# Turning the cluster similarities and the one-hot words on VectorE instead of on TensorE and by DMA

## The chip, the cores and the metric

The kernel runs on one core of one Trainium2 chip. The time is device time in microseconds (us) of that core for one execution. Before the change three runs gave 378.12, 378.9 and 383.21 us, a median of 378.9.

## The reference, cut to what matters

Two stages follow each other. The first is attention in which a query sees only the keys of its own cluster; the second is a gate with a long convolution, done by Fourier transforms (as matmuls in the kernel). The change lies in how the first finds the clusters.

```python
B, H, S, D, n_clusters = 4, 8, 768, 64, 16
q_assign = argmax(einsum('bhsd,hcd->bhsc', q_n, c_n), axis=-1)   # nearest of 16 centroids
k_assign = argmax(einsum('bhsd,hcd->bhsc', k_n, c_n), axis=-1)
mask     = q_assign[:, :, :, None] == k_assign[:, :, None, :]
scores   = where(mask, scale * q @ k.T, -1e9)
attn     = softmax(scores) @ v                                   # ties go to the first centroid
x        = attn, heads side by side                              # (4, 768, 512)
x1,x2,x3 = split(x @ w_proj)
out      = (x1 * irfft(rfft(x2) * rfft(filter)) * x3) @ w_out
```

The kernel makes no mask matrix. Each query and key gets 16 more rows beside its 64 features: a one-hot word of its cluster. A key's word is 1 at its cluster and 0 elsewhere, a query's is 0 at its cluster and a large negative number elsewhere, so the score matmul adds the mask by itself.

## The kernel before, in words

The 32 pairs of batch and head are worked in eight groups (n = 0 to 7) of four heads, each group in two pairs of heads (pr). `attention(n, pr)` (L677) runs over six tiles of 128 keys: TensorE (PE) makes the scores (L694, with the helper lines L82 and L84), ScalarE (ACT) their exponentials (L708, L711) into one of five p buffers, PE multiplies these with v (L718 to L725), and VectorE (DVE) adds them up for the denominators (L743; the first two tiles in thirds, on DVE or GpSimd (POOL), L739). `hyena(b)` (L831) is the second stage for batch b; its pieces are put between the attention of later groups, and the last batch's stand alone at the end. In it DVE multiplies spectra (L887), POOL or DVE combines them (L891), DVE and POOL unfold the inverse (L956, L966) and gate it (L969), and PE multiplies with w_out; the results go to `out` by DMAs of SP (L1012), two row tiles at a time (512 KB), except the very last tiles (L1008, L989).

`routing(n)` (L574) prepares group n, while group n - 1 is in attention:

- PE transposes raw q and k (L594), copies go to qkP (L282 on ACT, L284 on DVE), and casts of these to the bf16 tiles aug (L610, done on ACT, DVE or POOL).
- L625: 8 matmuls give the similarities in two PSUM banks, 128 partitions (4 blocks of 32: queries and keys of two pairs, 16 centroids for each of two heads) by 2 x 384 columns of tokens.
- L630: two copies, 128x384 fp32, by ACT or DVE, to the tile sim.
- L638: PE turns them with six fp32 128x128 transposes into two more banks, so that tokens lie on partitions.
- L646 and L648: DVE takes the maximum over 16 centroids and compares, from PSUM, once for each bank, into the tile oh.
- L651, L659, L663: ties are broken towards the first centroid (multiply by a falling weight, largest of 16 in four halvings), and the words made: L663 in two halves, `is_equal` for keys and `subtract` for queries.
- L668: one DMA transpose on SP turns oh back into ohT, with tokens along the row.
- L497, in `masks` (L490): eight DMAs on SP put rows of ohT into aug. The scores of group n wait for these.

Group 0 has its own path (`first_masks`, L502) and is left as it is.

The order on each engine is not the order of the code. `Plan.place` (L123) sorts all operations by a list schedule: each has an engine with a duration or several to choose from, what it reads and writes, and a due time. `NUDGE` (L42) shifts the due time of each operation, and `ONLY` (L43) pins 121 of them to an engine. The result is one fixed list for each engine. An operation with `lock` on POOL waits for the last such one on DVE. SP issues its DMAs in its own list's order, and each queue goes on only when its next entry is free to go.

Of the kernel before, what the change touches and what calls it, by code (L numbers as in the profile page):

```python
# [264 lines left out]
def build(T):  # L265
# [25 lines left out]
    def bank(i):  # L291
        return T.bank[i][:]
# [10 lines left out]
    def dma(e):  # L303
        return (T.nc.scalar if e == "ACT" else T.nc.sync).dma_start
# [269 lines left out]
    def routing(n):  # L574
# [54 lines left out]
        for ch in range(2):  # L629
            op(EV384, lambda e, ch=ch, h=h: copy(e, T.sim[:, ch], bank(h.ids[ch])[:, :384]), b0 + 1.4 + .1 * ch, r=[h],  # L630
               w=[("sim", ch, 0), ("sim", ch, 1)], free=[h])
        SIM = [("sim", ch, pr) for ch in range(2) for pr in range(2)]
        h = Bank(cls, 2)
        both = lambda x: [(x, 0), (x, 1)]

        def simT(e, h=h):
            for i in range(NT):
                T.nc.tensor.transpose(bank(h.ids[i // 3])[:, ts(i % 3, 128)], T.sim[:, i // 3, ts(i % 3, 128)],  # L638
                                      T.ident)
        op(("PE", .72), simT, b0 + 2.5, r=SIM + ["ident"], w=[h], alloc=h)  # L640

        words = lambda: T.oh[:].rearrange("p a n c -> p (a n c)").rearrange("p (m c i) -> p m c i", c=NC, i=4)
        for ch in range(2):
            sv = lambda ch=ch, h=h: bank(h.ids[ch])[:, :384].rearrange("p (m i c) -> p m i c", i=4, c=NC)
            mx = lambda ch=ch: T.mx[:, ch].rearrange("p (m i) -> p m i", i=4)
            op(("DVE", .55), lambda e, sv=sv, mx=mx: V().tensor_reduce(mx(), sv(), axis=AX, op=Alu.max),  # L646
               b0 + 3.3 + .2 * ch, r=[h], w=[("mx", ch)])
            op(("DVE", .55), lambda e, ch=ch, sv=sv, mx=mx: V().tensor_tensor(  # L648
                words()[:, 6 * ch:6 * ch + 6], sv().rearrange("p m i c -> p m c i"), mx().unsqueeze(2).to_broadcast([128, 6, NC, 4]),
                op=Alu.is_equal), b0 + 3.4 + .2 * ch, r=[h, ("mx", ch)], w=[("oh", ch)], free=[h])  # L650
# [627 lines left out]
```

## Time and profile before

| | |
|---|---|
| median of three runs | 378.9 us |
| the profiled execution | 378.54 us |
| its span on the core | 376.8 us |
| granted clock of PE, mean | 0.995 |
| PE busy | 363.2 us, 96% |
| DVE busy | 341.1 us, 91% |
| ACT busy | 263.9 us, 70% |
| POOL busy | 113.7 us, 30% |
| six transposes of L638, once for each of groups 1 to 7 | 42 matmuls of 273 ns (median), 0.81 to 0.82 us for six |
| DMA transposes of L668 | 7, of 1.25 to 1.69 us on SP, 2.8 us to landing |

A line of a group reads: the line of the kernel, engine and operation, what it writes and reads (partitions by elements, type), how often, then busy time in us, mean ns of one, and the idle time of the engine just before with what ended it. PE is TensorE's matmuls and PEld its weight loads, which lie beside them. A busy PE in this table is not the same as a PE at its peak, since the ends of matmuls are modelled. The chain of work that ended last goes back from the last instruction, at each step to what released it.

### The profile page before, as it was taken

Reading aid. Unit: us, or ns where it says so; the run is one execution under the profiler, and the core shown is the slowest. Engines: PE = TensorE matmul, PEld = TensorE weight load, DVE = VectorE, ACT = ScalarE, POOL = GpSimd, SP = SyncE. Lnnn points to the kernel's source line nnn. Section 1 sums busy time; section 2 is a strip of 40 time slices with the busy share of each in tenths; the row PEclk is TensorE's granted clock in tenths of the full one; section 3 lists DMA queues with packets and bytes.
Section 4 is the critical chain, followed back from the end, with each engine's and each line's share of the span. In section 5 each row is a group of like instructions: output and inputs, shape, how many; then the busy total and the mean of one; then the engine's idle time right before and its main releaser. Section 6 shows DMA issues by size and latency. Waiting matters only on the chain.

```text
span 376.8 us, 8529 instructions
## 1 busy us (share of the span) xinstructions
PE 363.2 (96%) x3253; PEld 209.1 (55%) x3257; DVE 341.1 (91%) x509; ACT 263.9 (70%) x492; POOL 113.7 (30%) x156
## 2 busy tenths in 40 slices
PE   6899998999999999999999999999999999999994
PEld 3454553554555664556556656576555666565672
DVE  7778997979999999998999998999998999999993
ACT  6997868984992879688869538878773588333332
POOL 8441103141204452122441134433121433024610
PEclk9899999999999999999999999999999999999999
DMA  9959669855766858539894877646467733110304
GB/s 171 167 138 199 107 139 224 177 105 116 178 139 125 174 68 169 67 103 179 148 149 130 150 176 175 145 64 90 75 115 179 144 66 69 46 43 0 159 11 167
DMA packets 95716, 47.56 MB, mean 126 GB/s; under 512 B 83816, under 2 KB 89660, under 8 KB 95676
## 3 DMA queue, kind: packets, MB, share of 16 engines
q1 hardware_dynamic: 91052, 37.39, 43.5%
q0 software_dynamic: 2752, 8.98, 16.8%
q10 hardware_dynamic: 1872, 0.66, 0.7%
q8 instruction: 25, 0.41, 0.5%
q14 instruction: 15, 0.12, 0.2%
HBM read 31.59 MB, written 7.40 MB: 103 GB/s over the span
## 4 chain that ended last, share of the span: by engine, by line
PE 69%; DVE 13%; ACT 7%; DMA 4%; issue 3%; SPq 2%; POOL 1%; DVEq 0%; POOLq 0%; ACTq 0%
PE pair L722 28%; PE bank L84 24%; PE bank L594 5%; PE bank L82 3%; PE bank L625 2%; PE bank L857 2%; DMA dn<-dd 2%; PE bank L638 2%; DVE tm L887 1%; DVE tm L871 1%; ACT aug L282 1%; SPq L497 1%; DMA aug<-ohT 1%; ACT p L711 1%; DMA dd<-acc 1%
## 5 line engine op out<-in xcount | busy, mean ns | idle before, releaser
L722 PE MATMUL pair<-p,vraw 128*64 128x385 f32 x768 | 142.4, 489 | 0.0
L711 ACT ACTIVATE p<-bank 128x512 f32<-128x512 f32 x192 | 108.5, 610 | 23.0 <-PE bank L84 20.2
L743 DVE TENSOR_TENSOR acc<-p,acc 128x1536 f32<-128x1536 f32 x64 | 113.5, 1774 | 10.9 <-POOL acc L739 5.8
L722 PEld LDWEIGHTS pair<-p,vraw 128*64 128x64 f32 x768 | 55.8, 136 | 46.3 <-issue 39.1
L84 PE MATMUL bank<-aug,aug 128*64 128x512 bf16 (+3 forms) x650 | 70.7, 325 | 1.4 <-DMA aug<-ohT 0.5
L708 ACT ACTIVATE p<-bank 128x512 f32<-128x512 f32 x96 | 57.9, 608 | 11.0 <-PE bank L84 8.3
L84 PEld LDWEIGHTS <-aug 128*64 128x64 bf16 (+1 forms) x650 | 39.6, 109 | 35.2 <-issue 24.8
L776 POOL DMA_DIRECT2D acc<-acc x30 | 23.7, 791 | 93.5 <-DMA acc<-acc 45.2
L84 PE MATMUL bank<-xT,wpj 128*64 128x384 bf16 x456 | 43.3, 326 | 0.0
L84 PEld LDWEIGHTS <-wpj 128*64 128x64 bf16 x456 | 27.7, 110 | 13.7 <-issue 5.2
L284 POOL CAST aug<-qkP 64x768 bf16<-64x768 f32 x23 | 19.3, 842 | 52.3 <-DVE acc L743 21.0
L739 POOL TENSOR_TENSOR acc<-p,p 128x512 f32<-128x512 f32 x14 | 18.1, 1297 | 48.5 <-DVE acc L739 26.0
L282 ACT COPY qkP<-bank 128x512 f32<-128x512 f32 (+1 forms) x47 | 23.8, 555 | 12.6 <-PE bank L594 8.7
L84 PEld LDWEIGHTS <-y 128*64 128x64 bf16 x472 | 23.8, 110 | 13.1 <-issue 4.0
L887 DVE TENSOR_TENSOR tm<-bank,hm 128x512 f32<-128x512 f32 x44 | 28.0, 680 | 1.5 <-POOL y L891 0.8
L891 POOL TENSOR_TENSOR y<-tm 128x512 bf16<-128x512 f32 x17 | 21.5, 1277 | 20.2 <-DVE tm L887 12.3
L282 ACT CAST aug<-qkP 64x768 bf16<-64x768 f32 x28 | 23.1, 830 | 1.4 <-PE bank L84 0.6
L84 PE MATMUL bank<-wout,y 128*64 128x512 bf16 (+1 forms) x200 | 23.4, 371 | 0.2 <-DVE y L969 0.2
L746 ACT COPY osb<-pair 128x770 f32<-128x770 f32 x16 | 12.9, 804 | 14.6 <-PE pair L722 14.4
L739 DVE TENSOR_TENSOR acc<-p,p 128x512 f32<-128x512 f32 x34 | 22.6, 693 | 0.3 <-ACT p L711 0.3
L857 PE MATMUL bank<-wpj,xT 128*64 128x512 bf16 x192 | 22.0, 379 | 0.0
L282 ACT COPY ob<-bank 128x512 f32<-128x512 f32 x20 | 11.1, 590 | 15.1 <-PE bank L84 13.1
(174 smaller groups left out, 457.8 us busy)
## 6 DMA issues: line engine op xcount, KB each, us to landing
vraw<-in_v_dram SPq DMA_DIRECT2D x16, 384.0 KB, 3.8
qkraw<-in_q_dram SPq DMA_DIRECT2D x30, 192.0 KB, 4.1
rb<-dr SPq DMA_DIRECT2D x30, 192.0 KB, 3.7
out_dram<-ob SPq DMA_DIRECT2D x11, 512.0 KB, 4.1
qkraw<-in_k_dram SPq DMA_DIRECT2D x29, 192.0 KB, 4.4
acc<-acc POOLq DMA_DIRECT2D x10, 384.0 KB, 5.0
acc<-acc POOLq DMA_DIRECT2D x10, 192.0 KB, 4.0
y<-in_moe_filter_fft_dram SPq DMA_DIRECT2D x4, 384.0 KB, 6.7
```

The costliest lines, as they stand in the source:

```text
L84: T.nc.tensor.matmul(out[64 * i:64 * i + 64], lhsT[:, 64 * i:64 * i + 64], rhs, start=start, stop=stop)
L282: T.nc.scalar.copy(out, in_)
L284: (T.nc.vector if e == "DVE" else T.nc.gpsimd).tensor_copy(out, in_)
L708: T.nc.scalar.activation(o, ap(h).rearrange("p (a b) -> p a b", a=2), Act.Exp, scale=0.125)
L711: T.nc.scalar.activation(flat(s)[:, lo:lo + 512], ap(h), Act.Exp, scale=0.125)
L722: T.nc.tensor.matmul(o[64 * hp:64 * hp + 64, ch, :385], T.vraw[vs][:, hp, sk * D:(sk + 1) * D], T.p[slots[sk]][:, hp, 384 * ch:384 * ch + ...
L739: alu(e).tensor_tensor(o, x, y, op=Alu.add)
L743: T.nc.vector.tensor_tensor(T.acc[os], T.p[slots[sk]][:, :, :S], T.acc[os], op=Alu.add)
L776: op(("POOL", .8), lambda e, rows=rows: T.nc.gpsimd.dma_start(flat_()[:rows], flat_()[rows:2 * rows], accum_op=Alu.add), te, r=[], w=AK, b ...
L857: T.nc.tensor.matmul(ap(h)[64 * i:64 * i + 64], T.xT[xs][:, kt, c:c + 64], T.wpj[:, kt, DM:2 * DM], start=kt == 0, stop=kt == ND - 1)
L887: op(("DVE", .68), lambda e, i=i, cs=cs, r=r, h=h: T.nc.vector.tensor_tensor(T.tm[r][:, cs], ap(h), hmrow(i, (0, 2, 2, 3)[2 * r + cs]), op ...
L891: op({"POOL": 1.5, "DVE": .68}, lambda e, i=i, r=r: alu(e).tensor_tensor(T.y[:, i, r], T.tm[r][:, 0], T.tm[r][:, 1], op=Alu.add if r else ...
```

## The change

For groups 1 to 7, tokens are no longer brought onto all 128 partitions. DVE transposes blocks of 32 by 32: two transposes read the similarities in PSUM and write sim, so that each block of 32 partitions holds 32 tokens, with their 16 centroids times two heads along the row. The views (`turned`) put the four blocks of 128 tokens side by side, so one step from centroid to centroid is four elements in sim and in oh. The copies of the similarities, the six PE transposes and their two banks go. The maximum and the comparison are made once over 768 elements, from sim in SBUF. The last step of the words is one `subtract` for queries and keys. A third DVE transpose turns oh into ohT in place of the DMA transpose, and a comparison with zero makes the keys' rows (partitions 64 to 127) 0 or 1. The rows that `masks` reads become 16 neighbouring partitions, where they were every fourth one.

In the last batch, the third and fourth output tiles are stored one by one as the fifth was, by SP or ACT.

`NUDGE` has new values for all operations, so that the order on every engine is new, and `ONLY` pins 96 in place of 121.

```diff
-NUDGE = {0:-457.288,1:-646.784,2:-12.57, ...
-ONLY = {10:"POOL",12:"POOL",13:"POOL", ...
+NUDGE = {0:-746.767,1:-4870.897,2:-1.564, ...
+ONLY = {10:"POOL",11:"POOL",13:"POOL", ...
@@ masks
-                    rows = slice(64 * j + 2 * pr + hp, 64 * j + 64, 4) if n else slice(64 * pr + 32 * j + 16 * hp, 64 * pr + 32 * j + 16 * hp + 16)
+                    rows = slice(*((64 * j + 32 * pr if n else 64 * pr + 32 * j) + 16 * hp + x for x in (0, 16)))
@@ routing
+        turned = lambda x, g: x.rearrange("p (g x i) -> p g i x", g=g, i=4)
         for ch in range(2):
-            op(EV384, lambda e, ch=ch, h=h: copy(e, T.sim[:, ch], bank(h.ids[ch])[:, :384]), b0 + 1.4 + .1 * ch, r=[h],
-               w=[("sim", ch, 0), ("sim", ch, 1)], free=[h])
+            op(("DVE", .55), lambda e, ch=ch, h=h: V().transpose(
+                turned(T.sim[:, ch], 3), bank(h.ids[ch])[:, :384].rearrange("p (g i x) -> p g i x", g=3, i=4)), b0 + 1.4 + .1 * ch,
+               r=[h], w=[("sim", ch, 0), ("sim", ch, 1)], free=[h])
-        h = Bank(cls, 2)
-        def simT(e, h=h):
-            for i in range(NT):
-                T.nc.tensor.transpose(bank(h.ids[i // 3])[:, ts(i % 3, 128)], T.sim[:, i // 3, ts(i % 3, 128)],
-                                      T.ident)
-        op(("PE", .72), simT, b0 + 2.5, r=SIM + ["ident"], w=[h], alloc=h)
-        words = lambda: T.oh[:].rearrange("p a n c -> p (a n c)").rearrange("p (m c i) -> p m c i", c=NC, i=4)
-        for ch in range(2):
-            sv = lambda ch=ch, h=h: bank(h.ids[ch])[:, :384].rearrange("p (m i c) -> p m i c", i=4, c=NC)
-            mx = lambda ch=ch: T.mx[:, ch].rearrange("p (m i) -> p m i", i=4)
-            op(("DVE", .55), lambda e, sv=sv, mx=mx: V().tensor_reduce(mx(), sv(), axis=AX, op=Alu.max),
-               b0 + 3.3 + .2 * ch, r=[h], w=[("mx", ch)])
-            op(("DVE", .55), lambda e, ch=ch, sv=sv, mx=mx: V().tensor_tensor(
-                words()[:, 6 * ch:6 * ch + 6], sv().rearrange("p m i c -> p m c i"), mx().unsqueeze(2).to_broadcast([128, 6, NC, 4]),
-                op=Alu.is_equal), b0 + 3.4 + .2 * ch, r=[h, ("mx", ch)], w=[("oh", ch)], free=[h])
+        flat3 = lambda x: x.rearrange("p (m c i) -> p m c i", c=NC, i=4)
+        sims = lambda: flat3(T.sim[:].rearrange("p a b -> p (a b)"))
+        words = lambda: flat3(T.oh[:].rearrange("p a n c -> p (a n c)"))
+        mx = lambda: T.mx[:].rearrange("p a (m i) -> p (a m) i", i=4)
+        op(("DVE", .93), lambda e: V().tensor_reduce(mx(), sims().rearrange("p m c i -> p m i c"), axis=AX, op=Alu.max),
+           b0 + 3.3, r=SIM, w=both("mx"))
+        op(("DVE", .93), lambda e: V().tensor_tensor(
+            words(), sims(), mx().unsqueeze(2).to_broadcast([128, 12, NC, 4]), op=Alu.is_equal), b0 + 3.4,
+           r=SIM + both("mx"), w=both("oh"), lock=True)
...
-        for j, o_ in ((1, Alu.is_equal), (0, Alu.subtract)):
-            op(("DVE", .36), lambda e, j=j, o_=o_: V().tensor_tensor(
-                words()[:, j::2], words()[:, j::2],
-                T.mt[:, :48].rearrange("p (m i) -> p m i", i=4)[:, j::2].unsqueeze(2).to_broadcast([128, 6, NC, 4]), op=o_),
-               b0 + 4.2, r=both("m2"), w=both("oh"), lock=True)
+        op(("DVE", .56), lambda e: V().tensor_tensor(
+            words(), words(), T.mt[:, :48].rearrange("p (m i) -> p m i", i=4).unsqueeze(2).to_broadcast([128, 12, NC, 4]),
+            op=Alu.subtract), b0 + 4.2, r=both("m2"), w=both("oh"), lock=True)
-        op(("SP", .6), lambda e: T.nc.sync.dma_start_transpose(
-            T.ohT[:].rearrange("p (t n) -> p t n", n=128), T.oh[:].rearrange("p a n c -> p (a n c)")), due - 2,
-           r=both("oh"), w=both("ohT"), byts=196e3, lat=3.0 if n < 3 else 1.0)
+        op(("DVE", .93), lambda e: V().transpose(
+            T.ohT[:].rearrange("p (g i x) -> p g i x", g=6, i=4), turned(T.oh[:].rearrange("p a n c -> p (a n c)"), 6)), due - 2,
+           r=both("oh"), w=both("ohT"), lock=True)
+        op(("DVE", .35), lambda e: V().tensor_scalar(T.ohT[64:], T.ohT[64:], 0.0, None, op0=Alu.is_equal), due - 1, r=[],
+           w=both("ohT"), lock=True)
@@ hyena
-                if last and tt == 2 and not e_:
-                    op(("SP", .4), lambda e, tt=tt, e_=e_, ob=ob: T.nc.sync.dma_start(
+                if last and tt and not (tt == 2 and e_):
+                    op({"SP": .4, "ACT": .4}, lambda e, tt=tt, e_=e_, ob=ob: dma(e)(
                         T.out[b].rearrange("(p t) m -> p t m", t=NT)[:, 2 * tt + e_], ob()[:, e_]), due + 2,
                        r=[obk[e_]], byts=157e3)
-            if not (last and tt == 2):
+            if not (last and tt):
...
-                   r=obk, byts=320e3)
+                   r=obk, byts=400e3)
```

More of the change, by code (lines that the diff above doesn't have):

```diff
@@ L43 @@
-ONLY = {10:"POOL",12:"POOL",13:"POOL",14:"POOL",15:"POOL",26:"SP",27:"SP",30:"SP",32:"ACT",34:"SP",38:"ACT",41:"ACT",50:"DVE",62:"ACT",64:"POOL",69:"POOL",90:"DVE",91:"POOL",94:"DVE",97:"DVE",98:"POOL",173:"POOL",174:"DVE",175:"DVE",223:"DVE",224:"DVE",229:"DVE",230:"POOL",235:"DVE",241:"ACT",242:"POOL",245:"ACT",323:"DVE",355:"POOL",357:"POOL",392:"ACT",405:"POOL",406:"DVE",408:"POOL",410:"DVE",411:"DVE",412:"DVE",414:"DVE",415:"POOL",419:"ACT",460:"POOL",462:"POOL",497:"DVE",512:"DVE",539:"DVE",547:"DVE",550:"DVE",563:"DVE",573:"ACT",580:"ACT",588:"ACT",595:"ACT",599:"DVE",607:"POOL",617:"ACT",687:"ACT",688:"ACT",689:"ACT",690:"DVE",692:"POOL",693:"DVE",695:"ACT",696:"DVE",697:"ACT",698:"POOL",699:"POOL",700:"ACT",701:"POOL",703:"DVE",704:"DVE",807:"POOL",808:"DVE",860:"ACT",861:"ACT",870:"ACT",915:"DVE",916:"DVE",988:"POOL",1010:"ACT",1048:"DVE",1051:"ACT",1066:"DVE",1068:"ACT",1095:"POOL",1146:"POOL",1147:"POOL",1152:"DVE",1154:"POOL",1155:"ACT",1156:"DVE",1312:"ACT",1313:"DVE",1314:"DVE",1315:"POOL",1317:"ACT",1372:"DVE",1419:"DVE",1424:"ACT",1452:"POOL",1492:"ACT",1500:"ACT",1505:"POOL",1519:"DVE",1603:"ACT",1604:"ACT",1605:"ACT",1610:"POOL",1611:"POOL",1612:"POOL",1770:"POOL",1772:"DVE",1882:"DVE",1889:"DVE",1934:"DVE",1939:"ACT",1942:"ACT"}
@@ new lines @@
+ONLY = {10:"POOL",11:"POOL",13:"POOL",15:"POOL",28:"SP",30:"ACT",31:"SP",33:"SP",35:"SP",41:"ACT",50:"DVE",62:"DVE",69:"POOL",92:"POOL",96:"DVE",98:"DVE",150:"DVE",173:"POOL",174:"DVE",175:"DVE",224:"POOL",229:"DVE",230:"DVE",235:"ACT",236:"POOL",241:"POOL",242:"ACT",354:"POOL",389:"ACT",402:"POOL",403:"ACT",404:"DVE",407:"DVE",409:"DVE",411:"ACT",412:"DVE",413:"POOL",454:"POOL",455:"POOL",456:"POOL",491:"DVE",556:"DVE",570:"DVE",578:"ACT",585:"DVE",604:"ACT",632:"POOL",681:"DVE",683:"DVE",685:"ACT",687:"DVE",692:"POOL",693:"POOL",694:"POOL",695:"POOL",799:"POOL",800:"POOL",851:"POOL",852:"POOL",853:"ACT",858:"POOL",903:"POOL",1006:"DVE",1007:"DVE",1009:"ACT",1013:"ACT",1037:"POOL",1043:"DVE",1050:"POOL",1051:"DVE",1064:"DVE",1131:"ACT",1132:"DVE",1135:"POOL",1142:"POOL",1297:"DVE",1300:"POOL",1301:"POOL",1302:"POOL",1303:"POOL",1308:"POOL",1311:"ACT",1406:"DVE",1493:"DVE",1506:"DVE",1594:"POOL",1595:"ACT",1630:"DVE",1750:"POOL",1899:"ACT",1907:"SP",1910:"DVE",1911:"SP",1914:"DVE",1915:"ACT",1918:"DVE"}
```

2 lines of the change are left out of this document (1 added, 1 removed).

## The prediction

> **What bounds the kernel now.** I read the busy shares first, then the windows by stage, then PE's own waits, and last the groups that the change touches.
>
> ```profile
> PE 363.2 (96%) x3253; PEld 209.1 (55%) x3257; DVE 341.1 (91%) x509; ACT 263.9 (70%) x492; POOL 113.7 (30%) x156
> ...
> PE 69%; DVE 13%; ACT 7%; DMA 4%; issue 3%; SPq 2%; POOL 1%; DVEq 0%; POOLq 0%; ACTq 0%
> ```
>
> PE is busy for 96% of the span and holds 69% of the chain that ended last. VectorE (DVE) is next with 91%. An average hides stages, so the windows:
>
> ```profile
> 0.00:25.00 25.00, 20.52 (x130) 10.82 (x132) 20.05 (x49) 21.25 (x40) 14.97 (x56) 0.93 0.89 175
> ...
> 60.00:110.00 50.00, 49.89 (x401) 25.10 (x404) 43.09 (x58) 40.92 (x79) 13.48 (x16) 1.00 0.70 154
> 110.00:160.00 50.00, 49.72 (x413) 28.11 (x411) 47.46 (x69) 36.56 (x66) 17.30 (x19) 1.00 0.69 122
> 160.00:210.00 50.00, 49.83 (x466) 29.39 (x465) 46.37 (x63) 42.19 (x78) 14.91 (x16) 1.00 0.76 144
> 210.00:230.00 20.00, 19.91 (x177) 11.83 (x173) 18.57 (x31) 9.34 (x17) 7.84 (x7) 1.00 0.79 177
> 230.00:300.00 70.00, 68.94 (x629) 41.87 (x629) 65.72 (x96) 49.59 (x93) 19.81 (x22) 1.00 0.63 119
> 300.00:330.00 30.00, 30.00 (x306) 18.62 (x304) 29.26 (x39) 20.07 (x39) 7.70 (x7) 1.00 0.25 57
> 330.00:376.80 46.80, 41.40 (x493) 25.96 (x489) 39.46 (x70) 16.37 (x32) 13.80 (x10) 1.00 0.20 77
> ```
>
> The columns are the length, then busy time of PE, PEld, DVE, ACT and POOL, the clock, the DMA share and GB/s. From 60 to 330 us PE is busy for 49.89 + 49.72 + 49.83 + 19.91 + 68.94 + 30.00 = 268.3 of 270 us at the full clock: there every us of PE work is a us of time. DVE is busy for 43.09 + 47.46 + 46.37 + 18.57 + 65.72 + 29.26 = 250.5 us of the same 270 (93%), so it has 19.5 us to give. Ahead of 60 us and behind 330 us no engine is full.
>
> **PE: what goes.** Each of groups 1 to 7 has six fp32 transposes of the similarities:
>
> ```profile
> L638 PE MATMUL bank<-ident,sim x42: 272/273/329, 36.0 to 273.2; 128*128 128x128 f32 x42
> ...
>   ACT sim L282: 1.5, 3
> ```
>
> In the chain of work in order of time the six stand as one piece of 0.81 or 0.82 us, and a group of eight matmuls of L722 takes 1.30 us, or 1.45 us right behind work of another array width. The seven pieces are 7 x 0.82 = 5.7 us. The built order of PE changes its array width 60 times in place of 76; one change at each block is in its 0.82, so about 9 more go, at 0 to 0.15 us each (1.45 - 1.30). I take 0.4 us. PE's saving is 6.1 us, between 5.7 and 7.1. The 1.5 us for which PE's weight load waited for the copies of the similarities is inside queues that PE overlaps; I count nothing for it. All other matmuls stay: more of them are issued as 64-wide pairs than as one 128-wide, and the chain has 8 of the one kind at 0.86 us (L84) and 4 of the other at 0.82 (L82), the same work for nearly the same time.
>
> **DVE: what goes and comes.** The rows:
>
> ```profile
> L648 DVE TENSOR_TENSOR oh<-bank,mx 128x384 bf16<-128x384 f32 x14 | 7.4, 553 | 0.3
> L646 DVE TENSOR_REDUCE mx<-bank 128x24 f32<-128x384 f32 x14 | 7.3, 548 | 0.7 <-PE bank L638 0.5
> ...
> L969 DVE TENSOR_TENSOR y<-yy,x 128x768 bf16<-128x768 f32 x7 | 6.7, 954 | 0.1
> ...
> L786 DVE TENSOR_REDUCE dn<-dp 128x12 f32<-128x192 f32 x10 | 4.9, 489 | 0.0
> ...
> L663 DVE TENSOR_TENSOR oh<-oh,mt 128x384 bf16<-128x384 bf16 x14 | 4.6, 351 | 0.2
> ```
>
> Removed in a group: two maxima at 0.548, two comparisons at 0.553, two steps of L663 at 0.351, so 2.90 us. Three of the 14 copies of the similarities were DVE's at 0.544, 1.6 us in all; the other 11 (0.481 each) leave ACT.
>
> Added in a group, if access order costs nothing: two transposes out of PSUM, 128x384 fp32, at the 0.548 of the other DVE reads of that shape (1.10); one maximum over 128x768 fp32 at L969's 0.954; one comparison at 0.954; one subtraction over 768 bf16 at the 0.561 of L651, its sister; the transpose of the words, 128x768 bf16, at 0.954; the comparison with zero on 64 partitions, bf16, 0.35 as L663 (up to 0.56 as L651). That is 4.87 us, and 4.87 - 2.90 = 1.97 us more a group.
>
> The bounds of the new ones: the transposes have no row. The cheapest they can be is the bf16 rate, L659's 0.354 for 384 elements and L651's 0.561 for 768, which is 0.2 and 0.4 us under my prices. The dear end is L786. It is a maximum's sister, a reduction whose elements lie 48 bytes apart, and takes 489 ns for 192 elements where L646 takes 548 for 384 in sequence. L340 (64 elements in sequence, 220 ns) and L646 make 1.03 ns an element and 155 ns fixed, so L786 needs (489 - 155) / 192 = 1.74 ns an element. The new maximum reads fp32 elements 16 bytes apart, the PSUM transposes write them 16 bytes apart, the transpose of the words reads bf16 8 bytes apart. At 1.74 ns the maximum costs 1.49 us (0.54 more), each PSUM transpose 0.82 (0.27 more), the words' transpose 1.49 (0.54 more). I take 1.49 for the maximum, since its row is near, and the low price for the transposes: the nearest strided write, L966's, runs backwards through its rows and takes 0.547 to 0.564 for 384 elements, as plain ones do. So a group costs 1.97 + 0.54 = 2.51 us more, between 1.97 - 2 x 0.2 - 0.4 = 1.2 and 1.97 + 0.54 + 2 x 0.27 + 0.54 + 0.21 = 3.8.
>
> The Trainium skill, "SBUF — State Buffer", section "Door 1: The DMA port swizzle", says that SBUF serves 16-byte lines and that an access which crosses to a new line each time pays for it; by that rule the maximum and the PSUM writes pay, the words' reads (two to a line) don't, and the sum for a group is the 3.05 us of 2.51 + 2 x 0.27. L786 agrees for reads, and no row here shows writes. The same notes, "VectorE: DVE Perf Modes", "The three transpose paths", give 311 ns for 128x128 bf16 on VectorE; three and six of those (an estimate) would make 0.93 and 1.87 us of my 0.55 and 0.95, and no run so far shows it.
>
> The new order moves other work off DVE. Counted in the built orders: 5 casts of 64x768 to ACT and POOL (2.7 us), two thirds of L739 to POOL (1.4), two sums of L764 to ACT (1.1), two qkP copies (1.2), one tm copy (0.7) less; one ob copy, one od copy, one L891, one L966 and one 256-column copy (2.9 together) more. Net -4.2 us. ACT loses 11 x 0.481 = 5.3 us and takes 3 casts (2.5) and two sums (1.0); POOL takes 1.9 us more on 30%. Neither fills.
>
> DVE from 60 to 330 us (six of the seven groups): 250.5 + 6 x 2.51 - 1.6 - 4.2 = 259.8 us in 270 - 5.6 = 264.4 us: 98%. Before, the fullest stretch that kept PE at 30.00 of 30 had DVE at 29.26 of 30, 97.5%. So DVE keeps up nearly, not quite. I charge 1.0 us of PE waiting, between 0 and the 9 that the second rival comes to.
>
> **Where a wait is added.** The copies of the similarities could go to either engine; now PE's two banks stay taken until DVE reaches its transposes. Behind a transpose that waits for PE stand L743 (1.77 us each) and the multiplications that free banks and p buffers, and ACT's exponentials wait for those buffers. This is in the 1.0 us.
>
> **DMA and queues.** Seven DMA transposes leave SP (1.25 to 1.69 us of issue, 2.8 us to landing). The last group's masks (eight DMAs, 6.35 us on SP from 284.76) follow the words after 4.3 us; then two DVE steps, 1.3 us, stand between. PE's only wait for masks:
>
> ```profile
> PE bank L84 <- DMA aug<-ohT: 0.5, 1, 0.5
> ```
>
> I count that 0.5 as gone, against 0.5 for the new order's own misfits. The masks' rows become adjacent partitions, with the same bytes and packets: nothing.
>
> **The tail.** The last store of a pair lands 4.1 us after issue (512 KB). The change splits the middle pair, but the first pair goes out last on SP, behind ACT's last 512-column copy. ACT then has three such copies (0.59) and one more DMA issue (about 0.56) ahead of its two final stores, in place of four and a 256-column one (0.39): 2.33 against 2.75 us at most. The last landings stay one 512 KB pair and two halves. I count 0, between -0.4 and +0.4; what hides it is the pair's 4.1 us.
>
> **Sum.** The profiled execution took 378.54 us (span 376.8 and 1.74 around it), 0.4 under the median of 378.9. 378.5 - 6.1 + 1.0 = 373.4 us.
>
> **The rivals.**
> DVE hidden: the maximum costs 0.95, DVE stands at 250.5 + 6 x 1.97 - 5.8 = 256.5 of 264 us (97%), and PE saves the upper 7.1 us, with 0.5 to 1 us from the earlier masks and the tail: about 370.7 us. For it: 300 to 330 us, where 97.5% held no one up. Against it: the L786 row.
>
> DVE becomes the bound, and the kernel is slower: every strided access pays 1.74 ns. A group then costs 1.97 + 1.62 = 3.59 us more, DVE needs 250.5 + 21.5 - 5.8 = 266.2 us, and it has waits of its own that need not shrink (in the table of waits 5.8 us for POOL's part of acc and 2.1 for ACT's p, of which I take 7): 273 us against 270 before, so 378.5 + 3 = 381.5 us. It decides from 270 - 7 = 263 us of DVE work, 3.1 us a group. Transposes at twice the element time would go further, 2 x 0.4 + 0.8 = 1.6 us a group beyond that, about 391 us.
>
> Nothing is gained: PE's 6 us go, but the new order opens gaps of as much at the start or the end, where before PE idles 4.5 and 5.4 us; 378 us. Against it: the instructions there are nearly the same.
>
> **Chances.** Forecast (371.3 to 376) 0.47; hidden 0.23; nothing gained 0.12; DVE bound at about 381.5 0.12, and worse 0.06. The range 369.5 to 382.0 holds most of these and leaves out the worst DVE case and the edges; the likeliest case's own is 371.3 to 376. A measurement here can tell about 2% from no change: under 371.3 is faster, over 386.5 slower. Faster 0.23, slower 0.06, same 0.71.
>
> **What would show it.** No L638; PE's busy time near 357 us, and above 99% from 60 us on. The maximum at 1.4 to 1.5 us (0.95 speaks for the hidden case), PSUM transposes near 0.55 (0.8 for the bound case), words' transpose near 0.95. DVE busy near 353 us. If PE's waits list DVE lines, or ACT's exponentials wait for acc, with several us, DVE is the bound and I am wrong; if PE idles at the start or the end, the order is.

## The result, and the profile after

The kernel after takes 389.61 us (median of 4 runs, 388.45 to 390.35) beside 378.51 us for the kernel before on the same chip: a ratio of 1.030 with a 95% interval of 1.026 to 1.034. Runs more than 1.5% above the fastest of the same kernel, here 383.21 us of before, are left out of the ratios. It is 3% slower; the prediction was 373.4 us, 1.4% faster, with a range to 382.0. The profiled execution of after took 388.45 us, its span 386.6 us, 9.8 us more than the span before.

The page of after, busy time and the chain that ended last:

```profile
PE 361.0 (93%) x3252; PEld 206.6 (53%) x3254; DVE 358.3 (93%) x506; ACT 264.2 (68%) x486; POOL 114.2 (30%) x158
...
PE 47%; DVE 37%; issue 7%; ACT 3%; DMA 2%; POOL 2%; SPq 1%; DVEq 0%; POOLq 0%; ACTq 0%
```

PE's share of the chain fell from 69% to 47%, VectorE's rose from 13% to 37%: the end hangs on VectorE almost as much as on PE. VectorE's busy time grew by 17.2 us (341.1 to 358.3).

The windows of after, columns as in the prediction (length, then busy time of PE, PEld, DVE, ACT, POOL, the clock, DMA share, GB/s):

```profile
60.00:110.00 50.00, 47.17 (x369) 23.37 (x370) 42.35 (x45) 40.11 (x76) 11.53 (x12) 0.94 0.55 123
110.00:160.00 50.00, 48.36 (x425) 26.96 (x422) 47.80 (x65) 36.42 (x66) 19.15 (x21) 1.00 0.73 134
160.00:210.00 50.00, 48.24 (x442) 28.82 (x442) 48.38 (x67) 37.22 (x68) 12.90 (x14) 1.00 0.64 110
210.00:230.00 20.00, 18.73 (x168) 10.69 (x166) 18.55 (x23) 13.71 (x28) 4.70 (x6) 1.00 0.73 170
230.00:300.00 70.00, 66.45 (x609) 39.65 (x608) 68.12 (x98) 48.90 (x87) 19.84 (x20) 1.00 0.62 125
300.00:330.00 30.00, 29.83 (x286) 18.83 (x282) 29.35 (x45) 20.68 (x40) 11.73 (x11) 1.00 0.43 70
```

Before, PE was full from 60 us on (49.83 of 50 us between 160 and 210). Now it lacks 1.3 to 3.6 us in each of the first five stretches, and from 160 to 300 us VectorE is at least as busy as PE (135.1 and 133.4 of 140 us). Only the stretch from 300 to 330 us looks as before.

The new groups on VectorE (busy us, then mean ns of one):

```profile
L631 DVE STREAM_TRANSPOSE sim<-bank 128x384 f32<-128x384 f32 x14 | 12.2, 942 | 0.1
L640 DVE TENSOR_REDUCE mx<-sim 128x48 f32<-128x768 f32 x7 | 11.0, 1576 | 0.2
L660 DVE STREAM_TRANSPOSE ohT<-oh 128x768 bf16<-128x768 bf16 x7 | 7.3, 1045 | 0.2
L642 DVE TENSOR_TENSOR oh<-sim,mx 128x768 bf16<-128x768 f32 x7 | 6.7, 953 | 0.1
...
L656 DVE TENSOR_TENSOR oh<-oh,mt 128x768 bf16<-128x768 bf16 x7 | 3.8, 546 | 0.1
L663 DVE TENSOR_SCALAR ohT<-ohT 64x768 bf16<-64x768 bf16 x7 | 2.5, 358 | 0.2
```

The PSUM transposes take 0.94 us where the sum had 0.55. The others are near their prices (1.58 for 1.49, 1.05 for 0.95, 0.953 for 0.954).

What PE waited for in after (us in total, times, longest), and its clock where the two longest gaps are:

```profile
PE bank L84 <- DVE x L923: 4.4, 5, 1.2
PE bank L750 <- DVE dn L783: 2.8, 1, 2.8
PE bank L82 <- DVE hm L455: 1.9, 2, 1.7
...
PE bank L84 <- DVE sim L631: 1.1, 4, 0.3
```

```profile
55.00:60.00 5.00, 2.67 (x15) 1.32 (x14) 5.00 (x8) 3.35 (x7) 0.00 (x0) 0.94 0.61 108
60.00:65.00 5.00, 5.00 (x32) 2.25 (x32) 3.50 (x4) 3.27 (x8) 2.64 (x4) 0.72 0.83 172
95.00:100.00 5.00, 2.78 (x18) 1.01 (x20) 4.97 (x6) 1.07 (x3) 2.51 (x2) 0.70 0.49 116
```

The waits are spread over many lines, most of them VectorE's, and most of those are steps that the change never touched (L923 sums x, L783 inverts denominators, L455 is the filter): they are late because of what stands ahead of them. In e1 below, where only the new steps are shorter, the wait for L923 falls from 4.4 to 1.1 us and that for L783 from 2.8 to 1.2. PE is idle for 16.0 us between 27 us and its end, 4.0 us before. Behind the gaps at 57 us (1.67 us) and 97 us (2.75 us) the clock records show half clock for 3.4 us each (of the stretch from 97 to 100 us the granted clock is 0.50). The mean clock fell from 0.995 to 0.987.

One mark splits the 9.8 us: the start of the sixteenth and last copy of an attention result (osb, on ACT). It stands at 331.5 us before and 338.2 after, 6.7 us later. From there to the end it is 45.3 us before and 48.4 after, 3.1 us more. The two stretches behind the mark, before and after:

```profile
331.48:376.80 45.32, 39.92 (x483) 25.45 (x479) 37.98 (x68) 15.89 (x31) 13.80 (x10) 1.00 0.21 79
338.25:386.60 48.35, 41.90 (x507) 27.82 (x503) 41.68 (x73) 15.20 (x30) 13.80 (x10) 0.97 0.20 75
```

PE has 2.0 us more work there (41.90 for 39.92), work that stands ahead of the mark in the old order. Only about 1 us of the 3.1 is added idle time of PE (6.4 for 5.4).

### The profile page after: what moved, and what is told of

Its sections match the earlier page's. It is cut to its first block, busy times and chain, and to the rows that moved or that the text cites. A ratio compares the mean times of both kernels' runs of the same rounds, so it can differ in the third digit from the quotient of the medians.

```text
span 386.6 us, 8526 instructions
## 1 busy us (share of the span) xinstructions
PE 361.0 (93%) x3252; PEld 206.6 (53%) x3254; DVE 358.3 (93%) x506; ACT 264.2 (68%) x486; POOL 114.2 (30%) x158
## 4 chain that ended last, share of the span: by engine, by line
PE 47%; DVE 37%; issue 7%; ACT 3%; DMA 2%; POOL 2%; SPq 1%; DVEq 0%; POOLq 0%; ACTq 0%
PE bank L84 21%; PE pair L716 18%; DVE acc L737 9%; DVE tm L881 2%; DVE acc L733 2%; PE bank L594 2%; DMA qkraw<-in_q_dram 2%; DVE mx L640 2%; DVE sim L631 2%; PE bank L82 1%; DVE tm L865 1%; DVE ohT L660 1%; PE bank L851 1%; ACT p L705 1%; DVE sd L950 1%
## 5 line engine op out<-in xcount | busy, mean ns | idle before, releaser
L737 DVE TENSOR_TENSOR acc<-p,acc 128x1536 f32<-128x1536 f32 x64 | 113.2, 1770 | 6.8 <-POOL acc L733 3.3
L84 PE MATMUL bank<-aug,aug 80*64 80x256 bf16 (+3 forms) x692 | 77.8, 330 | 6.5 <-DVE x L923 3.9
L84 PEld LDWEIGHTS <-aug 80*64 80x64 bf16 (+1 forms) x692 | 42.0, 110 | 46.6 <-issue 35.8
L84 PE MATMUL bank<-xT,wpj 128*64 128x384 bf16 x480 | 45.0, 326 | 1.1 <-ACT qkP L282 0.6
L284 POOL CAST aug<-qkP 64x768 bf16<-64x768 f32 x25 | 21.1, 847 | 58.5 <-DVE acc L737 20.5
L84 PEld LDWEIGHTS <-wpj 128*64 128x64 bf16 x480 | 30.0, 110 | 13.7 <-issue 4.6
L733 POOL TENSOR_TENSOR acc<-p,p 128x512 f32<-128x512 f32 x16 | 20.3, 1275 | 51.4 <-ACT p L705 23.9
L84 PEld LDWEIGHTS <-y 128*64 128x64 bf16 x488 | 25.5, 110 | 13.4 <-issue 5.0
L282 ACT CAST aug<-qkP 64x768 bf16<-64x768 f32 x31 | 25.4, 829 | 2.3 <-DVE qkP L284 1.7
L733 DVE TENSOR_TENSOR acc<-p,p 128x512 f32<-128x512 f32 x32 | 21.1, 688 | 2.9 <-ACT p L705 1.3
L594 PEld LDWEIGHTS bank<-ident,qkraw 128*128 128x128 f32 x144 | 15.5, 141 | 7.0 <-ACT p L705 2.4
```

What stands on the lines that cost most here:

```text
L84: T.nc.tensor.matmul(out[64 * i:64 * i + 64], lhsT[:, 64 * i:64 * i + 64], rhs, start=start, stop=stop)
L282: T.nc.scalar.copy(out, in_)
L284: (T.nc.vector if e == "DVE" else T.nc.gpsimd).tensor_copy(out, in_)
L594: T.nc.tensor.transpose(bank(h.ids[i // 4])[:, ts(i % 4, 128)], raw(ss[i // NT], i % NT), T.ident[:, ::-1] if 3 <= i < NT else T.ident)
L733: alu(e).tensor_tensor(o, x, y, op=Alu.add)
L737: T.nc.vector.tensor_tensor(T.acc[os], T.p[slots[sk]][:, :, :S], T.acc[os], op=Alu.add)
```

## The experiments

Two theories stood at the start. LENGTH: VectorE's new steps last longer than the order has room for. ORDER: the new order leaves gaps whatever they cost. Where an edit changes what is computed it is said; all other work is done in each. The time is the median; the ratio is that of the means, to runs of the kernel before on the same chip. In the table "last osb" is the mark of the section above, "behind it" the span less that mark. The last four columns are of the one profiled execution, which lies up to 3.4 us above its median (e7; 2.4 in e12, 1.3 in e3, 1.2 in e13) and down to 1.2 below it (after).

| run | time, us | ratio to before (95%) | DVE busy | span | last osb | behind it |
|---|---|---|---|---|---|---|
| before | 378.51 | 1 | 341.1 | 376.8 | 331.5 | 45.3 |
| after | 389.61 | 1.030 (1.026 to 1.034) | 358.3 | 386.6 | 338.2 | 48.4 |
| e1, copies, max in sequence | 380.14 | 1.004 (1.002 to 1.007) | 349.6 | 378.6 | 330.2 | 48.4 |
| e2, writes in sequence | 383.63 | 1.015 (1.011 to 1.019) | 353.9 | 381.7 | 333.4 | 48.3 |
| e3, max in sequence | 382.3 | 1.011 (1.007 to 1.015) | 353.5 | 381.8 | 333.4 | 48.4 |
| e4, both, compare strided | 386.69 | 1.022 (1.017 to 1.027) | 356.4 | 385.5 | 337.1 | 48.4 |
| e5, old order, no PE turns | 380.99 | 1.010 (1.008 to 1.012) | 347.6 | 379.1 | 333.8 | 45.3 |
| e6, old order, longer steps | 392.22 | 1.041 (1.037 to 1.045) | 356.1 | 389.9 | 344.6 | 45.3 |
| e7, e5 and e6 | 407.61 | 1.083 (1.078 to 1.088) | 365.8 | 409.3 | 364.0 | 45.3 |
| e8, after, two sums moved | 389.5 | 1.033 (1.029 to 1.036) | 358.1 | 388.5 | 340.1 | 48.4 |
| e9, e1 without tie steps | 376.0 | 0.996 (0.994 to 0.997) | 335.9 | 373.8 | 325.4 | 48.4 |
| e10, before without tie steps | 377.87 | 1.001 (0.999 to 1.003) | 327.3 | 377.0 | 331.7 | 45.3 |
| e11, e5 in sequence | 377.67 | 0.999 (0.997 to 1.002) | 345.3 | 376.3 | 331.0 | 45.3 |
| e12, after all in sequence | 380.51 | 1.009 (1.005 to 1.012) | 352.7 | 381.1 | 333.0 | 48.1 |
| e13, before, a third of the turns | 375.27 | 0.995 (0.993 to 0.997) | 340.9 | 374.7 | 329.4 | 45.3 |
| e14, e9 with a lighter end | 374.2 | 0.991 (0.988 to 0.994) | 334.9 | 372.4 | 324.4 | 48.0 |
| e15, e12 mended | 381.5 | 1.012 (1.009 to 1.015) | 351.8 | 378.7 | 330.9 | 47.8 |

**e1 to e4: the lengths, in the order of after.** Only the bodies of three steps change. e1 makes the transposes plain copies and lets the maximum read in sequence (clusters wrong):

```diff
-            V().transpose(turned(T.sim[:, ch], 3), bank(h.ids[ch])[:, :384]....)
+            V().tensor_copy(T.sim[:, ch], bank(h.ids[ch])[:, :384])
-            V().tensor_reduce(mx(), sims().rearrange("p m c i -> p m i c"), axis=AX, op=Alu.max)
+            V().tensor_reduce(T.mx[...], T.sim[...].rearrange("p a (n c) -> p (a n) c", c=NC), axis=AX, op=Alu.max)
```

> The changed kernel with its order kept, but the two transposes out of PSUM replaced by plain copies to sim in sequence, and the maximum reading sim in sequence (the clusters are then wrong, and so are the masks). Theory LENGTH: the 9.8 us came because the new VectorE steps are longer than the order allows for (two transposes 0.94 where 0.55 was planned, maximum 1.58 where 0.93 was planned). Then 14 x 0.39 + 7 x 0.62 = 9.8 us of VectorE work go and the time falls to 376 to 380 us. Theory ORDER: the new order itself leaves gaps, whatever the steps cost. Then the time stays within 2 us of 389.6.

e2 keeps the transposes, but writes them in sequence (clusters wrong): `V().transpose(T.sim[:, ch], bank(h.ids[ch])[:, :384])`.

> The changed kernel with its order kept; the two PSUM transposes write sim in sequence and no longer 16 bytes apart (columns are then in another order, so the clusters are wrong). If the step of the writes is what lengthens them, a transpose takes 0.55 to 0.60 us in place of 0.94, and by LENGTH the time falls by about 5 us, to 384 to 386. If turning itself is what costs, it stays at 0.9 and the time at 389. By ORDER the time stays within 2 us of 389.6 whatever the instruction takes.

e3 changes the maximum alone, as in e1 (clusters wrong).

> The changed kernel with its order kept; only the maximum reads sim in sequence (it then takes the maximum of the wrong elements). The maximum should take 0.95 us in place of 1.58. By LENGTH 7 x 0.62 = 4.3 us go, 384 to 387 us. By ORDER within 2 us of 389.6.

e4 has e2's transposes and e1's maximum, and computes the reference: the comparison reads in sequence and puts the words where the later steps want them, bf16 elements 8 bytes apart.

> The changed kernel with its order kept and another layout that computes the reference: transposes write sim in sequence, the maximum reads it in sequence, and the comparison writes the bf16 words 8 bytes apart. If a bf16 write 8 bytes apart costs nothing, the comparison stays at 0.95 and by LENGTH the time is as in the run with plain copies, 376 to 381 us; at 1.74 ns an element the comparison takes 1.49 and it ends 3 to 4 us above that. By ORDER within 2 us of 389.6.

Measured: e1 380.14 us, as LENGTH had it; 9.5 us of the time are lengths. Its groups:

```profile
L642 DVE TENSOR_TENSOR oh<-sim,mx 128x768 bf16<-128x768 f32 x7 | 7.4, 1057 | 0.1
L660 DVE STREAM_TRANSPOSE ohT<-oh 128x768 bf16<-128x768 bf16 x7 | 7.0, 995 | 0.2
L640 DVE TENSOR_REDUCE mx<-sim 128x48 f32<-128x768 f32 x7 | 6.6, 949 | 0.2
```

The maximum takes 0.949 us in sequence and 1.576 with elements 16 bytes apart. e2 and e3 came out 0.4 and 1.7 us under their ranges (383.63, 382.3). e4, at 386.69 us, came out 1.7 us over the dear end of LENGTH's range, 385, and its groups say why:

```profile
L642 DVE TENSOR_TENSOR oh<-sim,mx 128x768 bf16<-128x768 f32 x7 | 13.9, 1993 | 0.1
L631 DVE STREAM_TRANSPOSE sim<-bank 128x384 f32<-128x384 f32 x14 | 7.3, 555 | 0.1
```

Turning costs nothing beyond a copy: 0.555 us in sequence (0.545 for e1's copies). What costs is the stride, and e4 only moved it into the comparison: 1.99 us (median 1.89), where e12's comparison below, which reads the same way and writes in sequence, has a median of 0.95.

**e8: are the two gaps the loss?** After, with two sums of 1.75 us put behind what PE waits for; the same result.

```diff
     order = P.place({"PE": .3, "ACT": .8, "DVE": .8, "POOL": .8, "SP": .8}, banks_for)
+    for x, y in ((309, 151), (488, 392)):
+        order.remove(P.ops[x])
+        order.insert(order.index(P.ops[y]) + 1, P.ops[x])
```

> The kernel after, with two of its 1.75-us sums of L737 moved on VectorE: one behind the next three filter steps (L453, L455) that PE waits for at 57 us, one behind the L783 that PE waits for at 97 us. PE's gaps of 1.67 and 2.75 us should fall under 1.2 us, and with them both stretches of half clock (3.4 us each, 1.7 us lost in each). ORDER (these gaps are the loss): the time falls by 1.2 + 1.7 + 1.7 + 1.7, about 6 us, to 383 to 384.5. LENGTH (VectorE is late all the way, a gap closed here opens later): it falls by 1 to 4 us, to 386 to 388.5.

Measured: 389.5 us, as after. PE's waits in e8:

```profile
PE bank L84 <- DVE x L923: 4.3, 5, 1.2
PE bank L750 <- DVE acc L737: 2.1, 2, 1.8
PE bank L82 <- DVE qkP L284: 2.0, 1, 2.0
```

At 57 us PE no longer waits for the filter, but for the next thing in VectorE's line, the copies qkP (gap 2.05 us); at 97 us for the moved sum itself (1.77 us). The half clock still stands behind both:

```profile
60.00:65.00 5.00, 5.00 (x30) 2.17 (x29) 3.55 (x4) 3.02 (x6) 2.51 (x4) 0.66 0.79 160
95.00:100.00 5.00, 3.55 (x26) 1.84 (x28) 4.96 (x6) 2.52 (x6) 2.51 (x2) 0.76 0.41 110
```

So e8 did not close the gaps, and it can't say what closing them would bring. It shows that what stands next in VectorE's line there is late too. What speaks against ORDER in the form of these two gaps is e1. It keeps the gap of 1.67 us at 57 us and loses as much to half clock there as after does in both places:

```profile
55.00:60.00 5.00, 3.05 (x12) 1.27 (x11) 5.00 (x8) 3.00 (x6) 0.00 (x0) 0.73 0.59 106
60.00:65.00 5.00, 5.00 (x27) 2.18 (x27) 3.19 (x4) 2.79 (x7) 2.76 (x4) 0.59 0.92 192
```

That is (0.27 + 0.41) x 5 = 3.4 us, and yet its span is 8.0 us shorter than that of after.

**e5, e6, e7, e11: the old order.** e5 leaves PE's transposes out of before; maximum and comparison read the copies in SBUF (clusters wrong). e6 issues each maximum and each comparison twice. e7 does both. e11 is e5 with the comparison reading in sequence.

```diff
-                T.nc.tensor.transpose(bank(h.ids[i // 3])[:, ts(i % 3, 128)], T.sim[:, i // 3, ts(i % 3, 128)], T.ident)
+                pass
-            sv = lambda ch=ch, h=h: bank(h.ids[ch])[:, :384].rearrange("p (m i c) -> p m i c", i=4, c=NC)
+            sv = lambda ch=ch, h=h: T.sim[:, ch].rearrange("p (m i c) -> p m i c", i=4, c=NC)
...
-               V().tensor_reduce(mx(), sv(), axis=AX, op=Alu.max)
+               [V().tensor_reduce(mx(), sv(), axis=AX, op=Alu.max) for _ in range(2)]
```

> The kernel before, in its old order, without the 42 fp32 transposes of the similarities on PE; the maxima and comparisons read the copies in SBUF instead (so the clusters are not those of the reference; all other work is done). It asks what the removed PE work was worth. If PE is what sets the time from 60 to 330 us, all of 7 x 0.82 = 5.7 us comes back: 371.5 to 373.5 us. If VectorE, at 93%, holds the end by itself, less than 2 us comes back: above 376.

> The kernel before, in its old order, with every maximum and every comparison of groups 1 to 7 issued twice: 7 x 2 x (0.548 + 0.553) = 15.4 us more of VectorE work, about the 17 us by which VectorE's busy time grew from before to after; PE's work unchanged. LENGTH (longer VectorE steps hold PE up wherever they stand): 384 to 390. ORDER (the old order has VectorE's spare time where the steps are, the new order has not): 378 to 381.

> Both edits: the kernel before without the 42 PE transposes and with the maxima and comparisons twice, so about the PE and VectorE work of the kernel after, in the old order. LENGTH: 380 to 386, since the PE saving is worth less once VectorE is late. ORDER: 372 to 376.

> e5_no_pe_turns again, but the comparisons read the copies in sequence, so that VectorE's steps last as in the kernel before (0.55 us each; in e5 the comparison took 1.08 us from SBUF with a step of 64 bytes where from PSUM it takes 0.55). PE's 5.7 us are gone and VectorE's busy time is as before, 341 us. VECTORE (only the longer steps hid the PE saving): 371.5 to 374 us. If VectorE's unchanged 341 us hold the end by themselves: 376 to 378.

e6 is the clean one, since it changes lengths alone: 392.22 us, over the dear end of LENGTH's range. VectorE's busy time grew by 15.0 us (341.1 to 356.1), the span by 13.1. PE's first wait names the step:

```profile
PE bank L84 <- DVE oh L648: 7.5, 7, 2.0
PE bank L82 <- DVE oh L648: 1.8, 2, 1.2
```

So the old order had no room for it either, though VectorE shows 91% there. The doubled steps also hold PE's PSUM banks longer, and both lines are waits for such a bank: e6 prices longer steps at this place of the order, and not VectorE work anywhere. e5 and e7 were missed by far (381 for at most 378, 408 for at most 386), mainly because the comparison changed its length with its source; e7 also ran at a mean clock of 0.960. The rows of the comparison in e5 and of the maximum beside it (shortest, median, longest, in ns):

```profile
L647 DVE TENSOR_TENSOR oh<-sim,mx x14: 784/814/2790, 36.4 to 277.7; 128x384 bf16<-128x384 f32 x14
L645 DVE TENSOR_REDUCE mx<-sim x14: 534/540/554, 35.5 to 276.5; 128x24 f32<-128x384 f32 x14
```

The comparison reads 64 bytes apart: from PSUM its median was 557 ns, from SBUF 814, and five of the 14 took over 1 us, one of them 2.79. e11 reads in sequence (median 557 ns) and still has one of 2.60 us. Its timeline there, on VectorE and on POOL:

```profile
183.00 2.60 DVE L647 TENSOR_TENSOR oh<-sim,mx 128x384 bf16<-128x384 f32 x1
```

```profile
182.93 2.25 POOL L965 TENSOR_TENSOR yy<-sd 128x384 f32<-128x384 f32 x2
```

The step with both inputs in SBUF ended only when POOL's two instructions had ended, 0.42 us behind the second (at 185.60 and 185.18 us). e11's 377.67 us lies where VectorE was to hold the end by itself (376 to 378). But VectorE's busy time is not the unchanged 341 us of that expectation, it is 345.3, so e11 doesn't price the PE work by itself; e13 was made for that.

**e9, e10: VectorE relieved.** e9 is e1 without the steps that settle ties (L645, L653, L656), e10 is before without its own (L651, L659, L663); clusters wrong in both.

```diff
-        op(("DVE", .56), lambda e: V().tensor_tensor(words(), words(), T.revx..., op=Alu.mult), b0 + 4, ...)
+        op(("DVE", .56), lambda e: None, b0 + 4, ...)
...
-                V().tensor_tensor(y, x[:, :, :n_], x[:, :, n_:], op=Alu.max)
```

> The kernel after with the new VectorE steps made cheap as in e1_plain (copies in place of the turning transposes, the maximum in sequence) and without the steps that settle ties (L645, L653, L656: 2.1 us a group, 14.8 us in all); so the clusters are wrong, all other work is done. VectorE's busy time falls to about 335 us. In the runs so far of the new order the span was VectorE's busy time and 28 to 29 us more. VECTORE (it sets the time, and PE's saving is real but hidden behind it): the time falls until PE is full, to what the prediction's sum gives without its charge, 370.5 to 373.5 us. ORDER or a PE saving worth nothing: 376 to 379.

> The kernel before without the same steps that settle ties (here 0.56 + 1.00 + 2 x 0.351 = 2.26 us a group, 15.8 us in all; clusters wrong): VectorE's busy time falls from 341 to about 325 us, PE's work is the same. If PE sets the time of the old order, 376 to 378.5 us, nearly nothing gained, and the gain of e9 over this one is the price of the removed PE work (about 5 to 6 us). If VectorE had a share in the old order's time, below 374.

The busy times of e9 and of e10:

```profile
PE 357.4 (96%) x3254; PEld 205.6 (55%) x3254; DVE 335.9 (90%) x464; ACT 263.3 (70%) x486; POOL 115.1 (31%) x158
```

```profile
PE 362.0 (96%) x3257; PEld 212.3 (56%) x3257; DVE 327.3 (87%) x460; ACT 264.1 (70%) x492; POOL 113.1 (30%) x156
```

e10 behaved as expected: 13.8 us less VectorE work in the old order bring nothing (ratio 1.001). e9 was missed by VECTORE: 376.0 us, at the edge of what ORDER expected. The last osb comes at 325.4 us, 6.1 us earlier than before, and 3.1 us more follow it. That 6.1 is also the saving of the prediction's sum is in part luck: the new order has 2.0 us less PE work ahead of the mark and as much more behind it (41.90 us busy there, as in after). Over the whole run PE's busy time fell by 5.8 us (363.2 to 357.4), and its idle time grew by 2.8 (13.6 to 16.4 us, the span less the busy time); that leaves 3.0.

**e13, e14: PE's work alone, and the end.** e13 keeps two of each group's six PE transposes in the kernel before (clusters wrong), so that no step of VectorE changes. e14 gives two copies in the end of e9 to ACT (as e9, clusters wrong).

```diff
+                if i % 3 == 0:
                     T.nc.tensor.transpose(bank(h.ids[i // 3])[:, ts(i % 3, 128)], ...)
```

```diff
+    for x in (1493, 1506):
+        P.ops[x].on = "ACT"
```

> The kernel before with 2 of the 6 PE transposes of each group left and 4 left out (clusters wrong); the maxima and comparisons read the same PSUM banks as before, so no VectorE step changes. In e5 and e11 they read SBUF, and some of them took 2.6 us beside POOL's L965. PE loses 28 transposes, 4/6 of 5.7 us, 3.8 us. PE (the old order's time is PE's work): 373.5 to 375 us. VECTORE or ACT next in line at once: 376.5 to 378.

> e9_after_relieved with two copies behind the last PV (one of 384 columns of x, one of 512 columns of ob; 0.55 and 0.68 us) given to ACT, which is busy for 19 of the last 48 us. The end of the new order has 41.9 us of VectorE work in its 48.2 us, the old one 38.2 in 45.2. END (VectorE sets the end, and the new order left it 3.7 us more there): 1.0 to 1.4 us less than e9, 374.6 to 375.1 us. If PE or the stores set it: no change, 376.0 within 0.3.

e13: 375.27 us beside 377.38, 2.1 us less, just outside the range for PE. The 3.8 us that the range starts from are too many, since the transposes overlap. One group's, in before (L638) and in e13 (L639):

```profile
72.91 0.88 PE L638 MATMUL bank<-ident,sim 128*128 128x128 f32 x6
```

```profile
72.16 0.44 PE L639 MATMUL bank<-ident,sim 128*128 128x128 f32 x2
```

Leaving out four takes 0.44 us off a group, 3.1 in all. PE's busy time fell by 2.4 us (363.2 to 360.8), the span by 2.1. So in the old order what PE's busy time loses is nearly all time; where the other 0.7 of the 3.1 us went was not followed. e14: 374.2 us, a little under the range, but not where it should be: the stretch behind the last osb fell from 48.4 to 48.0 us, the rest of the difference lies ahead of it, where e14 changes nothing. The profiled execution of e9 lost up to 1.7 us to half clock between 5 and 15 us (granted clock 0.71 from 10 to 15), that of e14 none, and e14's runs in the ratio lie between 371.9 and 375.9. That VectorE sets the end is not shown.

**e12, e15: the same result with every step in sequence.** The words stay in the order in which the 32 by 32 blocks come out; only the subtraction repeats its second operand. e15 adds the edits of e8 and e14.

```diff
-                turned(T.sim[:, ch], 3), bank(h.ids[ch])[:, :384].rearrange("p (g i x) -> p g i x", g=3, i=4))
+                T.sim[:, ch], bank(h.ids[ch])[:, :384])
-        words = lambda: flat3(T.oh[:].rearrange("p a n c -> p (a n c)"))
+        words = lambda: T.oh[:].rearrange("p a n c -> p (a n) c")
-            T.ohT[:].rearrange("p (g i x) -> p g i x", g=6, i=4), turned(T.oh[...], 6))
+            T.ohT[:], T.oh[:].rearrange("p a n c -> p (a n c)"))
```

> The kernel after, computing the same result, with every VectorE step of the words in the order in which the 32 by 32 blocks come out: transposes, maximum, comparison, weights, halvings and the transpose back all in sequence; only the subtraction reads its second operand repeated 16 times in place of in sequence. VectorE by e1's rows: 0.556 x 2 + 0.95 + 0.95 + 0.56 + 1.0 + 0.95 + 1.0 + 0.36 = 6.9 us a group in place of 7.9, busy time 351 to 352. VECTORE: its busy time and 28 to 29 us, and 1.9 around the span: 381 to 382.5 us. If the repeated operand costs more than 0.95 (as e4's comparison did, 1.99): up to 389.

> e12_all_in_sequence (computes the reference) with the two copies of e14 given to ACT and the two sums of e8 moved. The end: 1.2 us less. The moved sums: nothing if VectorE is the bound all the way (as in e8), up to 1.67 + 1.7 us less if the gap at 57 us and its half clock go and VectorE catches up. So 376 to 379.5 us, against 380.5 of e12 and 377.7 of the kernel before.

e12's groups:

```profile
L640 DVE TENSOR_TENSOR oh<-sim,mx 128x768 bf16<-128x768 f32 x7 | 7.4, 1051 | 0.1
L630 DVE STREAM_TRANSPOSE sim<-bank 128x384 f32<-128x384 f32 x14 | 7.3, 556 | 0.1
...
L638 DVE TENSOR_REDUCE mx<-sim 128x48 f32<-128x768 f32 x7 | 6.7, 950 | 0.2
L654 DVE TENSOR_TENSOR oh<-oh,mt 128x768 bf16<-128x768 bf16 x7 | 6.6, 945 | 0.1
```

380.51 us, half a us under its range, with every step near its price: 8 to 9 us less than after (by the ratios and by the medians), but still 0.9% (0.5 to 1.2) slower than before. e15 missed its range by 2 us: 381.5, no better than e12. No kernel here that computes the reference beats the kernel before. An order laid out for the measured lengths was not tried: that of after, which all of e1 to e4, e9 and e12 keep, was made with 0.55 us for a PSUM transpose and 0.93 for the maximum.

## Why the prediction was wrong, point by point

**PE's saving, 6.1 us: right in size.** PE's busy time in e9 is 5.8 us below that of before, and by e13 such a cut is time in the old order (2.1 us of span for 2.4 us of busy time). In after it is buried: PE waits longer, and is itself busy for 361.0 us, 3.6 more than in e9.

**The step that failed: "it has 19.5 us to give", and so the charge of 1.0 us for PE waiting.** In the runs of the new order in which VectorE is busy for 349 us or more, the span less VectorE's busy time is 29.0 (e1), 27.8 (e2), 28.3 (e3), 29.1 (e4), 28.4 (e12) and 28.3 us (after), and 30.4 (e8) and 26.9 (e15) where pieces were moved. So the span follows VectorE nearly one for one: from e1 to after it grows by 8.0 us for 8.7 of VectorE work. In the old order 15.0 us more cost 13.1 (e6, at the place of its steps). The 93% in the window table was therefore no spare time. VectorE's idle pieces lie where it waits itself (in before 5.8 us for POOL's part of acc, 2.1 for ACT's p, 1.7 for a DMA), and PE waits for VectorE at many small places, not for a sum over 270 us. That a step which comes at another moment can't use those pieces is argued from the waits and was not tested by itself.

e2 has just the steps of the prediction's sum (transposes at 0.556, maximum 1.65, words' transpose 1.00; VectorE busy for 353.9 us, in the sum 353). It takes 383.6 us, 10.2 over the forecast. PE is idle for 21.8 us of its span (381.7 less 359.9), in the kernel before for 13.6 (376.8 less 363.2). That is 8.2 us where the sum charged 1.0, and half clock takes up to 1.8 us more (granted clock 0.80 and 0.85 in the two stretches from 55 to 65 us). Even e1, whose 349.6 us of VectorE work are less than the sum's, is 6.7 us over the forecast.

Taking VectorE work off soon stops paying. e9 has 13.7 us less VectorE work than e1, and its span is 4.8 us shorter; 3.4 of these are the half clock that e1 has and e9 doesn't have from 55 to 65 us.

**Prices on VectorE: one of them wrong.** The PSUM transposes were taken at 0.548 us because L966 writes backwards at no cost. That was the wrong row: backward elements still lie side by side, turned ones 16 bytes apart. They measure 0.942, so 14 x 0.39 = 5.5 us; e2 without it is 6.0 us faster than after. The maximum, priced by L786's stride, was near (1.576 for 1.49), the words' transpose too (1.045 for 0.954; its median is 0.978). VectorE's busy time came to 358.3 us in place of 353. The Trainium skill, "SBUF — State Buffer", section "Door 1: The DMA port swizzle", which the prediction cited and did not follow, says that an access which crosses to a new 16-byte line each time pays for it; by that rule the transposes' writes and the maximum's reads pay and the words' reads, two to a line, don't. The transposes' 0.942 against 0.556, the maximum's 1.576 against 0.949 and the words' median of 0.978 in after and in e12 alike agree with it.

**The moved work and the end, priced at 0.** The new order leaves 41.7 us of VectorE work and 41.9 of PE work behind the last osb, in place of 38.0 and 39.9 (busy time behind the mark; one sum L737 and two copies of ob are the largest part of VectorE's). This stretch is 2.8 to 3.1 us longer in every run of the new order, and 2.5 to 2.7 where e14's two copies are moved. 2.0 us of that are PE work that only stands on the other side of the mark; about 1 us is added idle time of PE. So the "nothing gained" rival's gaps at the end are there, but at a sixth of the 6 us that it gave them. Which of the two engines makes it long, and whether the single stores share in it, stays open; that change was not tried by itself.

**The clock** was not in the sum. The two stretches of 3.4 us at half clock in after lose up to 1.7 us each; the kernel before and e9 have none there. They are not what separates after from e1, which loses as much. What closing the gaps ahead of them would bring stays open, since e8 only moved them.

**The rivals.** "DVE becomes the bound" was the right mechanism and was given 0.12, at 381.5 us; its worse form, transposes at twice the element time, about 391, comes nearest to the 389.6 measured, but by luck: it has the words' transpose at twice its price too, which measured 1.045 for 0.954, and VectorE full, where after has 254.6 us of VectorE work in the 270 from 60 to 330 us. It was held unlikely because the stretch from 300 to 330 us ran PE full with VectorE at 97.5%. That stretch was no measure for the others: even in after it keeps PE at 29.83 of 30, while 60 to 110 us, with VectorE at only 42.35 of 50, lacks 2.83 us.

**The sum as it was:** 376.8 (span before) - 5.8 (PE work that went, by e9's busy time) + 3.6 (PE busy for longer, up to 3.4 of it by half clock) + 12.0 (PE idle: 25.6 us in after, 13.6 before) = 386.6 us. e1's edits, which take away the strides of two steps, bring back 8.0 of it (378.6).

## What to carry to other kernels

In a kernel tuned until two engines are nearly full, neither's idle share need be spare: lengthen one step (as e6 does) before you trust a 93%. Here added work on the second engine cost nearly its whole price, while taking 13.8 us away from it in the old order (e10) gained nothing. Price a strided access by a row with that stride in that memory, and not by one that merely looks irregular. When work is taken off the bound, follow one mark inside the run as well as the end, and count the work on both sides of it: here 2.0 of the 6.1 us at the mark were work that had moved behind it.

## What the runs showed of the hardware

- Strides on VectorE, medians. fp32, 384 elements: writing to SBUF 16 bytes apart 0.884 us (L631 of after) against 0.550 in sequence (e2); reading from SBUF 64 bytes apart 0.814 (e5) against 0.557 in sequence (e11), the same read from PSUM 0.557 (before). 768 elements: reading fp32 16 bytes apart 1.577 (after) against 0.953 (e1); e4's comparison, which writes bf16 8 bytes apart, 1.891 against 0.951 in sequence (e12). (By the rule of 16-byte lines of the Trainium skill that is cited above this last one, two elements to a line, would be free; the measured 1.891 decides.)
- A VectorE step with both inputs in SBUF that started 0.07 us after a POOL step lasted until POOL was through, 2.60 us for 0.56 (e11). The Trainium skill, "SBUF — State Buffer", section "Who interferes with whom", says that a VectorE instruction with two SBUF inputs contends with a GpSimd instruction that reads SBUF, over a shared port pair that works as an exclusive lock; the two lines above agree. The second of POOL's two instructions started 0.89 us after the VectorE step, and the step still ended behind it; why is not shown.
- Half clock for about 3.4 us came behind PE gaps of 1.67 and 2.75 us (after) and 2.05 and 1.77 us (e8), and for 6.8 us behind one of 1.67 us (e1). It did not come behind gaps of 2.03 us at 38 us, 1.69 at 101 and 1.80 at 194 in e6 (granted clock 1.00). The length of the gap alone doesn't decide.
